# One reciprocal for the softmax sums of up to three head pairs, spread back through DRAM, in an attention plus two feed-forward kernel

## Chip, cores and metric

The kernel runs on one core of a Trainium2 chip. The metric is the device time in microseconds (us) of one execution, as the median of several runs; lower is better. The core has five engines that each work through their own list of instructions in order: TensorE (PE; its weight loads are listed apart as PEld), VectorE (DVE), ScalarE (ACT), GpSimd (POOL) and SyncE (SP), which here only issues DMA transfers. Engines wait for each other through semaphores.

## What is computed

```python
scores = q @ k.T / sqrt(64)                 # batch 2, 12 heads, 448 tokens, head size 64
scores = cap * tanh(scores / cap)
attn   = exp(scores - max(scores))          # the kernel leaves the max out: softmax does not depend on it
attn   = attn / (sum(attn) + 1e-9)
x = (attn @ v)                              # heads side by side: 896 tokens x 768
h = x @ w_in;  g = s * relu(h)**2 + b;  x = g @ w_out          # 768 -> 2048 -> 768
h = x @ w2_in; g = h * clip(h + 3, 0, 6) / 6; y = g @ w2_out   # 768 -> 2048 -> 768
```

## The kernel before

**Attention.** The 24 heads are taken in 12 pairs; pairs 0 to 5 belong to batch entry 0, pairs 6 to 11 to entry 1. A pair has four units, one for each block of 112 keys. For a unit n, `scores` (L211) writes keys by queries for both heads into a PSUM tile `ps`; `tanh` (L215) and `exps` (L220) on ACT make the tile `t` in SBUF; `attend` (L228) multiplies it with v and adds into the PSUM tile `pav` of the pair; `add_up` (L236) adds the four `t` of a pair into `acc`, the first add on POOL, the other two on DVE. `total` (L246) multiplies `acc` with a matrix of ones, so that all 64 rows of a head in the PSUM tile `pz` hold the same sums over the keys. `invert` (L251) takes the reciprocal of the whole tile, 128 rows by 448, into `rb`; `scale_x` (L255) multiplies `pav` with it; `split_x` (L260, L261) parts the product into a rounded half `xh` and a rest `xl`, which the feed-forward products need.

**Feed-forward.** `products` (L100) multiplies every weight block three times (rest of w by xh, w by xl, w by xh) into a PSUM tile `pf`. The weights come as 64-bit numbers in 68 chunks; each is fetched by SP (L57) into `raw`, then made into two fp32r halves by `rescale` (ACT, L64), `join` in three steps (DVE, L76, L78, L80), `upper` (ACT, L89) and `lower` (DVE, L95). The first two chunks are prepared beside the attention, one step every third unit (the table `early`).

**Order.** The order of instructions on every engine is the order in which the code is written (`manual_schedule`); the loop over n is a software pipeline. At step n it issues `scores(n+2)`, `exps(n)`, `tanh(n+1)`, then, where n is 4p+6, `total(p)` and `invert(p)`, then `attend(n-1)` and `add_up(n-1)`, and at n = 4p+8 `scale_x(p)` and `split_x(p)`. From n = 47 on it also issues two pieces of the feed-forward a step; a piece is three matmuls. The first twelve pieces (half of two weight chunks) read x of batch entry 0 only; the next twelve read x of entry 1, pair 6 first, pair 11 sixth. The joins of the third chunk are issued beside the first twelve pieces. SP's queue holds the loads of q and k (L203) of the pairs to come and the fetches of weights, in the order of the code. The buffers that matter: `pav` 3, `pz` 1, `t` 6, `acc` 2, `rqk` 3.

Of the kernel before, what the change touches and what calls it, by code (L numbers as in the profile page):

```python
# [7 lines left out]
F32 = mybir.dt.float32  # L8
# [15 lines left out]
WARM = 2  # L24
SCALE = 1.0 / D**0.5


@with_exitstack
def attention_moe_moe(ctx: ExitStack, tc: tile.TileContext, qk, v, cap, w1i, w1o, s, b, w2i, w2o, out):
    nc = tc.nc  # L30
    const = ctx.enter_context(tc.tile_pool(name="const", bufs=1))
# [9 lines left out]
    zeros = tp.tile([128, S], F32, name="zeros", tag="h")  # L41
    ones = const.tile([QT, D], F32, name="ones")
    x = [[act.tile([128, KD, S], F32R, name=f"x{p}{bi}") for p in ("h", "l")] for bi in range(B)]
# [205 lines left out]
    def invert(p):
        rb[p] = at.tile([128, S], F32, name="rb", bufs=2)  # L250
        nc.vector.reciprocal(rb[p], sums.pop(p)[:, :S])  # L251

    def scale_x(p):
        xf[p] = at.tile([128, S], F32, name="xf", bufs=2)
        nc.vector.tensor_mul(xf[p], pav.pop(p)[:, :S], rb.pop(p))  # L255

    def split_x(p):
        bi, hp = divmod(p, H // 2)
        hi, lo = (t[:, hp, :] for t in x[bi])
        nc.vector.tensor_copy(hi, xf[p])  # L260
        nc.vector.tensor_sub(lo, xf.pop(p), hi.bitcast(F32))  # L261

    with tc.manual_schedule():
# [24 lines left out]
        early = {6 + 3 * j: step for j, step in enumerate(steps + [(rescale, 2)])}  # L288

        fill, ps_f = None, None  # L290
        has = lambda n: 0 <= n < N
        for n in range(-2, N + 5):
# [71 lines left out]
```

## Time and profile before

| | us |
|---|---|
| median of 3 runs (lowest, highest) | 586.85 (586.08, 587.51) |
| the profiled execution | 586.05 |
| its span, first to last instruction | 584.3 |
| attention, until the feed-forward runs alone | about 0 to 124 |
| feed-forward alone | about 124 to 584 |

| engine | busy us | share of the span |
|---|---|---|
| PE | 569.6 | 97% |
| DVE | 403.1 | 69% |
| ACT | 272.7 | 47% |
| POOL | 31.1 | 5% |

How to read it: a share over the whole span mixes the two stages, so the stage of the attention is read by itself, from the waits and the lists in order of time. Times in those lists count from the start of the span. In a row, the bracket at the end gives the idle time of the engine before the instruction and what ended it. An instruction of DVE can begin while the last one still drains, so the time that one costs its queue is the distance between two starts, a little less than its own length.

### The profile page before, as it was taken

The numbers are of one execution on the slowest core, as the hardware profiler recorded it, in microseconds if no ns is written. First come the engines' busy times: TensorE is split into PE (matmuls) and PEld (weight loads), VectorE is DVE, ScalarE is ACT, GpSimd is POOL, SyncE is SP. The second block draws the span as 40 slices with busy tenths as digits, with TensorE's granted clock in tenths as the row PEclk, the third lists the DMA queues.
The fourth block names the chain that finished last, engine by engine and source line by source line (L and its number), as shares of the span: only waits on it lengthen the run. The fifth ranks groups of instructions, "written<-read, shape, count | busy, mean of one in ns | idle before, by whom it ended". The sixth has DMA issues, their size and how long they took to land.

```text
span 584.3 us, 6908 instructions
## 1 busy us (share of the span) xinstructions
PE 569.6 (97%) x2740; PEld 459.7 (79%) x2740; DVE 403.1 (69%) x521; ACT 272.7 (47%) x386; POOL 31.1 (5%) x16
## 2 busy tenths in 40 slices
PE   7998898999999999999999999999999999999997
PEld 2222222489999999999999999999999999999996
DVE  1699999998777777564456457888888864455420
ACT  6988878455555555223222325555555522321210
POOL 1221423100000000000000000000000000000000
PEclk9999999999999999999999999999999999999999
DMA  8903220033333323432343323333332344433200
GB/s 266 274 31 118 63 70 16 1 108 109 108 109 108 109 90 109 145 97 90 102 146 92 115 100 108 109 108 109 108 109 91 108 145 130 161 116 121 67 33 31
DMA packets 14097, 61.77 MB, mean 106 GB/s; under 512 B 1826, under 2 KB 3618, under 8 KB 13842
## 3 DMA queue, kind: packets, MB, share of 16 engines
q1 hardware_dynamic: 13920, 61.12, 32.1%
q8 instruction: 21, 0.34, 0.2%
q10 hardware_dynamic: 146, 0.23, 0.1%
q14 instruction: 10, 0.08, 0.0%
HBM read 58.59 MB, written 2.75 MB: 105 GB/s over the span
## 4 chain that ended last, share of the span: by engine, by line
PE 79%; DVE 13%; ACT 5%; issue 2%; DMA 1%; ACTq 0%; DVEq 0%
PE pf L100 78%; DVE acc L236 5%; DVE rb L251 5%; ACT t L215 2%; ACT t L220 2%; DVE xf L255 1%; DMA rqk<-in_qk 1%; DVE xh L260 1%; DVE w L80 0%; DVE w L78 0%; DVE xl L261 0%; PE ps L211 0%; PE pz L246 0%; DVE wlo L95 0%; ACT raw L64 0%
## 5 line engine op out<-in xcount | busy, mean ns | idle before, releaser
L100 PE MATMUL pf<-xh,wlo 128*128 128x448 f32 x384 | 140.7, 366 | 0.0
L100 PE MATMUL pf<-xl,whi 128*128 128x448 f32 x384 | 140.3, 365 | 0.2 <-DVE xl L261 0.2
L100 PE MATMUL pf<-gh,whi 128*128 128x448 f32 x384 | 140.2, 365 | 0.0
L100 PE MATMUL pf<-gl,whi 128*128 128x448 f32 x384 | 140.2, 365 | 0.0
L100 PE MATMUL pf<-xh,whi 128*128 128x448 f32 x384 | 140.2, 365 | 0.0
L100 PE MATMUL pf<-gh,wlo 128*128 128x448 f32 x384 | 140.2, 365 | 0.0
L89 ACT CAST whi<-w 128x768 fp32r<-128x768 f32 (+1 forms) x68 | 54.2, 798 | 175.1 <-PE pf L100 96.8
L95 DVE TENSOR_TENSOR wlo<-w,whi 128x768 fp32r<-128x768 f32 (+1 forms) x68 | 61.6, 906 | 82.9 <-ACT whi L89 82.9
L100 PEld LDWEIGHTS pf<-xh,wlo 128*128 128x128 f32 x384 | 72.1, 188 | 8.6 <-issue 2.8
L100 PEld LDWEIGHTS pf<-xl,whi 128*128 128x128 f32 x384 | 72.1, 188 | 6.1 <-DVE xl L261 0.5
L100 PEld LDWEIGHTS pf<-gh,whi 128*128 128x128 f32 x384 | 72.1, 188 | 5.7
L100 PEld LDWEIGHTS pf<-gl,whi 128*128 128x128 f32 x384 | 72.1, 188 | 5.7
L100 PEld LDWEIGHTS pf<-xh,whi 128*128 128x128 f32 x384 | 72.1, 188 | 5.7
L100 PEld LDWEIGHTS pf<-gh,wlo 128*128 128x128 f32 x384 | 72.1, 188 | 5.7
L78 DVE SCALAR_TENSOR_TENSOR w<-raw,w 128x768 uint32<-128x768 uint32 (+1 forms) x68 | 61.9, 911 | 2.3
L80 DVE SCALAR_TENSOR_TENSOR w<-raw,w 128x768 uint32<-128x768 uint32 (+1 forms) x68 | 61.9, 911 | 2.3
L64 ACT ACTIVATE raw<-raw 128x768 f32<-128x768 f32 (+1 forms) x68 | 58.8, 865 | 0.0
L211 PE MATMUL ps<-rqk 64*112 64x448 f32 x192 | 48.2, 580 | 1.8 <-ACT t L215 1.0
L215 ACT ACTIVATE t<-ps 112x896 f32<-112x896 f32 x48 | 43.5, 907 | 12.4 <-PE ps L211 12.4
L236 DVE TENSOR_TENSOR acc<-acc,t 112x896 f32<-112x896 f32 x24 | 41.3, 1721 | 10.3 <-POOL acc L236 9.2
L220 ACT ACTIVATE t<-t 112x896 f32<-112x896 f32 x48 | 45.6, 949 | 1.4
L228 PE MATMUL pav<-t,va 112*64 112x448 f32 x192 | 46.1, 559 | 0.0
(35 smaller groups left out, 355.2 us busy)
## 6 DMA issues: line engine op xcount, KB each, us to landing
raw<-in_w1i SPq DMA_DIRECT2D x16, 768.0 KB, 4.2
raw<-in_w2i SPq DMA_DIRECT2D x16, 768.0 KB, 4.3
raw<-in_w1o SPq DMA_DIRECT2D x12, 768.0 KB, 4.2
raw<-in_w2o SPq DMA_DIRECT2D x12, 768.0 KB, 4.3
rqk<-in_qk SPq DMA_DIRECT2D x11, 448.0 KB, 4.4
raw<-in_w1o SPq DMA_DIRECT2D x6, 512.0 KB, 3.8
raw<-in_w2o SPq DMA_DIRECT2D x6, 512.0 KB, 3.9
out<-y SPq DMA_DIRECT2D x12, 224.0 KB, 1.9
```

The source lines that it names most:

```text
L64: nc.scalar.activation(up, up, AF.Copy, scale=2.0**-112)
L78: nc.vector.scalar_tensor_tensor(out=bits, in0=up, scalar=0x80000000, in1=bits, op0=ALU.bitwise_and, op1=ALU.bitwise_or)
L80: nc.vector.scalar_tensor_tensor(out=bits, in0=low, scalar=29, in1=bits, op0=ALU.logical_shift_right, op1=ALU.bitwise_or)
L89: nc.scalar.copy(ready[i][0][:, :n], whole[i][:, :n])
L95: nc.vector.tensor_sub(lo[:, :n], whole.pop(i)[:, :n], hi[:, :n].bitcast(F32))
L100: nc.tensor.matmul(ps[:, :S], w[a][:, sl], rhs[r], start=(k == 0 and i == 0), stop=(k == n_k - 1 and i == 2))
L211: nc.tensor.matmul(ps[:, j, :S], raw_qk[p][rows, 1, c * QT:(c + 1) * QT], raw_qk[p][rows, 0, :], start=True, stop=True)
L215: nc.scalar.activation(u_t[n], u_ps.pop(n)[:, :, :S], AF.Tanh, scale=icap_r)
L220: nc.scalar.activation(u_t[n], u_t[n], AF.Exp, scale=cap_r)
L228: nc.tensor.matmul(pav[p][D * j:D * j + D, :S], va[bi][:, 2 * hp + j, c, :], u_t[n][:, j, :], start=(c == 0), stop=(c == NQ - 1))
L236: (nc.gpsimd if c == 1 else nc.vector).tensor_add(acc[p], u_t.pop(n - 1) if c == 1 else acc[p], u_t[n])
L251: nc.vector.reciprocal(rb[p], sums.pop(p)[:, :S])
```

## The change

- The pairs are put in groups of 3, 3, 3, 2 and 1 (`GROUPS`). `total` multiplies `acc` with a matrix that has ones only in every n-th column (`pick`), and the pairs of a group add into the same `pz`: row i of a head's 64 rows holds the sums of pair i modulo n. One reciprocal then serves the whole group (`invert`, 5 instead of 12).
- The reciprocals of a group lie in n rows for each head. Two DMA transfers on SP write these rows to DRAM, and two more read them back, each repeated over 64 partitions, into a tile `rb` of 128 x (n x 448). For the group of one nothing is spread.
- `take` copies `pav` to an SBUF tile `xu` as soon as the pair's products are complete, at n = 4p+6. `pav` has 2 buffers instead of 3.
- `finish_x` multiplies in place and makes xh and xl. For the pairs of a group whose last pair is q it is issued at n = 4q+8, 4q+10 and 4q+12, for the last group at n = 51.
- The first add of a pair's four units goes to DVE too. POOL only fills `pick` at the start.

```diff
+GROUPS = [(0, 3), (3, 3), (6, 3), (9, 2), (11, 1)]
...
-    ps_v = tc.alloc_tile_pool(name="ps_v", bufs=3, space=PSUM)
+    ps_v = tc.alloc_tile_pool(name="ps_v", bufs=2, space=PSUM)
...
-        (nc.gpsimd if c == 1 else nc.vector).tensor_add(acc[p], u_t.pop(n - 1) if c == 1 else acc[p], u_t[n])
+        nc.vector.tensor_add(acc[p], u_t.pop(n - 1) if c == 1 else acc[p], u_t[n])
...
+            nc.tensor.matmul(sums[p0][D * j:D * j + D, :S], pick[:, PICKS.index((n, p - p0)), :], acc[p][:, j, :], start=(p == p0), stop=(p == p0 + n - 1))
...
+    def take(p):
+        xu[p] = at.tile([128, S], F32, name="xu", bufs=5)
+        nc.vector.tensor_copy(xu[p], pav.pop(p)[:, :S])
+    def invert(p0):
+        n = group[p0][1]
+        rz[p0] = at.tile([128, S], F32, name="rz", bufs=2)
+        nc.vector.reciprocal(rz[p0], sums.pop(p0)[:, :S])
+        if n == 1:
+            rb[p0] = rz[p0]
+            return
+        rows = dram.tile([2, n, S], F32, name="rows", bufs=2)
+        wide = at.tile([128, 3, S], F32, name="rb", bufs=2)
+        for j in range(2):
+            nc.sync.dma_start(rows[j], rz[p0][D * j:D * j + n, :])
+        for j in range(2):
+            nc.sync.dma_start(wide[D * j:D * j + D, :n, :], rows[j:j + 1].to_broadcast([D, n, S]))
+        for r in range(n):
+            rb[p0 + r] = wide[:, r, :]
+    def finish_x(p):
...
+        xf = xu.pop(p)
+        nc.vector.tensor_mul(xf, xf, rb.pop(p))
+        nc.vector.tensor_copy(hi, xf)
+        nc.vector.tensor_sub(lo, xf, hi.bitcast(F32))
...
             if part == 0 and 0 <= done < P:
                 total(done)
-                invert(done)
+                if done == sum(group[done]) - 1:
+                    invert(group[done][0])
             if has(n - 1):
                 attend(n - 1)
                 add_up(n - 1)
-            if part == 2 and 0 <= done < P:
-                scale_x(done)
-                split_x(done)
+            if part == 0 and 0 <= done < P:
+                take(done)
+            for p in finishes.get(n, ()):
+                finish_x(p)
```

The line numbers of the changed kernel are higher: L240 is the add, L258 `take`, L263 the reciprocal, L270 and L272 the transfers to DRAM and back, L280 to L282 `finish_x`; L78, L80, L82 and L97 are the joins and `lower` that were L76, L78, L80 and L95. PE's list of instructions is the same but for `pick`, and ACT's is the same.

DVE's list around the reciprocal of the third pair, before:

```order
L251 RECIPROCAL rb<-pz 128x448
L236 TENSOR_TENSOR acc<-acc,t 112x896
L80 SCALAR_TENSOR_TENSOR w<-raw,w 128x768
L236 TENSOR_TENSOR acc<-acc,t 112x896
L255 TENSOR_TENSOR xf<-pav,rb 128x448
L260 CAST xh_74<-xf 128x448
L261 TENSOR_TENSOR xl_75<-xf,xh_74 128x448
L251 RECIPROCAL rb<-pz 128x448
```

And after:

```order
L263 RECIPROCAL rz<-pz 128x448
L240 TENSOR_TENSOR acc<-t 112x896
L258 COPY xu<-pav 128x448
L240 TENSOR_TENSOR acc<-acc,t 112x896
L82 SCALAR_TENSOR_TENSOR w<-raw,w 128x768
L240 TENSOR_TENSOR acc<-acc,t 112x896
L280 TENSOR_TENSOR xu<-xu,rb 128x448
L281 CAST xh_74<-xu 128x448
L282 TENSOR_TENSOR xl_75<-xu,xh_74 128x448
L240 TENSOR_TENSOR acc<-t 112x896
L258 COPY xu<-pav 128x448
L280 TENSOR_TENSOR xu<-xu,rb 128x448
```

A third add and the copy of `pav` have come in behind the reciprocal, the first multiplication by `rb` stands behind them, and the adds of the next pair but one stand behind that multiplication.

SP's list from the load of v for batch entry 1 (`va_95`) on, before:

```order
L274 DMA va_95<-in_v 112x3072
L203 DMA rqk<-in_qk 128x896 x4
L57 DMA raw<-in_w1i 128x1536
L203 DMA rqk<-in_qk 128x896 x4
L57 DMA raw<-in_w1i 128x1536
L203 DMA rqk<-in_qk 128x896
```

And after (`va_97` is the same load):

```order
L295 DMA va_97<-in_v 112x3072
L207 DMA rqk<-in_qk 128x896 x3
L270 DMA rows<-rz 3x448 x2
L272 DMA rb<-rows 64x1344 x2
L207 DMA rqk<-in_qk 128x896
L59 DMA raw<-in_w1i 128x1536
L207 DMA rqk<-in_qk 128x896 x2
L270 DMA rows<-rz 3x448 x2
```

The four small transfers of a group stand in the same queue as the loads; the load of the next pair's q and k comes behind them.

DVE's list at the end of the attention, from the reciprocal of pair 10 (here the sums of pairs 9 and 10), before:

```order
L251 RECIPROCAL rb<-pz 128x448
L236 TENSOR_TENSOR acc<-acc,t 112x896 x2
L255 TENSOR_TENSOR xf<-pav,rb 128x448
L260 CAST xh_76<-xf 128x448
L261 TENSOR_TENSOR xl_77<-xf,xh_76 128x448
L76 TENSOR_SCALAR w<-raw 128x768
L78 SCALAR_TENSOR_TENSOR w<-raw,w 128x768
L80 SCALAR_TENSOR_TENSOR w<-raw,w 128x768
L251 RECIPROCAL rb<-pz 128x448
L95 TENSOR_TENSOR wlo<-w,whi 128x768
L255 TENSOR_TENSOR xf<-pav,rb 128x448
L260 CAST xh_76<-xf 128x448
```

And after, from the first multiplication by the spread `rb` on:

```order
L280 TENSOR_TENSOR xu<-xu,rb 128x448
L281 CAST xh_76<-xu 128x448
L282 TENSOR_TENSOR xl_77<-xu,xh_76 128x448
L78 TENSOR_SCALAR w<-raw 128x768
L80 SCALAR_TENSOR_TENSOR w<-raw,w 128x768
L82 SCALAR_TENSOR_TENSOR w<-raw,w 128x768
L263 RECIPROCAL rz<-pz 128x448
L258 COPY xu<-pav 128x448
L280 TENSOR_TENSOR xu<-xu,rb 128x448
L281 CAST xh_76<-xu 128x448
L282 TENSOR_TENSOR xl_77<-xu,xh_76 128x448
L280 TENSOR_TENSOR xu<-xu,rz 128x448
```

The last reciprocal, that of pair 11, has moved behind the multiplication of pair 9, which reads what the DMA brings; behind it now stand a copy and the work on two pairs (10 and 11) instead of one, and `lower` has moved to the end.

## Rows read from the trace of the kernel before

**Rows 1.** The page, busy us (share of the span) xinstructions.

```profile
PE 569.6 (97%) x2740; PEld 459.7 (79%) x2740; DVE 403.1 (69%) x521; ACT 272.7 (47%) x386; POOL 31.1 (5%) x16
```

**Rows 2.** PE's waits, 20 to 110 us: us in total, times, longest.

```profile
PE pz L246 <- DVE acc L236: 7.4, 7, 1.5
```

**Rows 3.** PE in order of time: start us, us, instruction [idle before].

```profile
1.39 3.35 PE L280 MATMUL pz<-zeros 128*128 128x448 f32 x4 [1.39 <-DVE zeros L275]
...
19.48 0.97 PE L246 MATMUL pz<-acc,ones 112*64 112x448 f32 x4
...
35.81 0.97 PE L246 MATMUL pz<-acc,ones 112*64 112x448 f32 x4
...
99.56 0.97 PE L246 MATMUL pz<-acc,ones 112*64 112x448 f32 x4 [1.01 <-DVE acc L236]
107.89 0.97 PE L246 MATMUL pz<-acc,ones 112*64 112x448 f32 x4 [1.08 <-DVE acc L236]
...
123.89 0.47 PE L100 MATMUL pf<-xl,whi 128*128 128x448 f32 x1 [0.19 <-DVE xl L261]
```

**Rows 4.** DVE in order of time, same columns, in the attention.

```profile
20.50 2.96 DVE L251 RECIPROCAL rb<-pz 128x448 f32<-128x448 f32 x1 [5.54 <-PE pz L246]
23.38 2.22 DVE L236 TENSOR_TENSOR acc<-acc,t 112x896 f32<-112x896 f32 x2
25.52 0.61 DVE L255 TENSOR_TENSOR xf<-pav,rb 128x448 f32<-128x448 f32 x1
...
59.01 3.92 DVE L236 TENSOR_TENSOR acc<-acc,t 112x896 f32<-112x896 f32 x2
62.86 0.61 DVE L255 TENSOR_TENSOR xf<-pav,rb 128x448 f32<-128x448 f32 x1
63.50 0.39 DVE L260 CAST xh<-xf 128x448 fp32r<-128x448 f32 x1
63.93 0.63 DVE L261 TENSOR_TENSOR xl<-xf,xh 128x448 fp32r<-128x448 f32 x1
64.47 2.95 DVE L251 RECIPROCAL rb<-pz 128x448 f32<-128x448 f32 x1
67.34 1.03 DVE L236 TENSOR_TENSOR acc<-acc,t 112x896 f32<-112x896 f32 x1
68.28 0.55 DVE L76 TENSOR_SCALAR w<-raw 128x768 uint32<-128x768 uint32 x1
```

**Rows 5.** DVE in order of time, end of the attention.

```profile
116.00 0.55 DVE L76 TENSOR_SCALAR w<-raw 128x768 uint32<-128x768 uint32 x1
...
117.58 0.96 DVE L80 SCALAR_TENSOR_TENSOR w<-raw,w 128x768 uint32<-128x768 uint32 x1
118.46 2.95 DVE L251 RECIPROCAL rb<-pz 128x448 f32<-128x448 f32 x1
...
123.21 0.62 DVE L261 TENSOR_TENSOR xl<-xf,xh 128x448 fp32r<-128x448 f32 x1
```

**Rows 6.** A load of four bytes and the DVE instruction that waits for it.

```profile
0.73 0.52 ACTq L264 DMA_DIRECT2D capt<-in_cap  x1
...
1.97 0.15 DVE L281 RECIPROCAL icap<-capt 1x1 f32<-1x1 f32 x1 [0.56 <-DMA capt<-in_cap]
```

**Rows 7.** The page, DMA issues: xcount, KB each, median us to landing.

```profile
raw<-in_w1i SPq DMA_DIRECT2D x16, 768.0 KB, 4.2
...
out<-y SPq DMA_DIRECT2D x12, 224.0 KB, 1.9
```

**Rows 8.** Short stretches, per engine busy us; last PEclk, DMA share, GB/s.

```profile
21.00:21.50 0.50, 0.50 (x4) 0.27 (x4) 0.50 (x1) 0.50 (x1) 0.00 (x0) 1.00 1.07 246
21.50:22.00 0.50, 0.50 (x4) 0.00 (x0) 0.50 (x1) 0.50 (x2) 0.00 (x0) 1.00 0.72 172
...
120.50:121.00 0.50, 0.50 (x4) 0.47 (x3) 0.50 (x1) 0.50 (x2) 0.00 (x0) 1.00 0.92 381
```

**Rows 9.** The page, granted TensorE clock in 40 slices, tenths.

```profile
PEclk9999999999999999999999999999999999999999
```

More of the change, by code (lines that the diff above doesn't have):

```diff
@@ L25 @@
 SCALE = 1.0 / D**0.5
+GROUPS = [(0, 3), (3, 3), (6, 3), (9, 2), (11, 1)]
+PICKS = [(n, r) for n in (1, 2, 3) for r in range(n)]
 @with_exitstack
@@ L41, in attention_moe_moe @@
     zeros = tp.tile([128, S], F32, name="zeros", tag="h")
-    ones = const.tile([QT, D], F32, name="ones")
+    pick = const.tile([QT, len(PICKS), D], F32, name="pick")
     x = [[act.tile([128, KD, S], F32R, name=f"x{p}{bi}") for p in ("h", "l")] for bi in range(B)]
@@ L187, in attention_moe_moe @@
     at = tc.alloc_tile_pool(name="at", bufs=3)
-    ps_v = tc.alloc_tile_pool(name="ps_v", bufs=3, space=PSUM)
+    dram = ctx.enter_context(tc.tile_pool(name="dram", bufs=2, space=bass.MemoryType.DRAM))
+    ps_v = tc.alloc_tile_pool(name="ps_v", bufs=2, space=PSUM)
     ps_z = tc.alloc_tile_pool(name="ps_z", bufs=1, space=PSUM)
@@ L192, in attention_moe_moe @@
     N, P = len(units), B * H // 2
-    raw_qk, u_ps, u_t, acc, pav, sums, rb, xf = {}, {}, {}, {}, {}, {}, {}, {}
+    group = {p: (p0, n) for p0, n in GROUPS for p in range(p0, p0 + n)}
+    raw_qk, u_ps, u_t, acc, pav, xu, sums, rz, rb = {}, {}, {}, {}, {}, {}, {}, {}, {}
     va = [at.tile([QT, H, NQ, D], F32, name=f"va{bi}", bufs=1) for bi in range(B)]
@@ L242, in total @@
     def total(p):
-        sums[p] = ps_z.tile([128, 512], F32, name="pz")
+        p0, n = group[p]
+        if p == p0:
+            sums[p0] = ps_z.tile([128, 512], F32, name="pz")
         for j in range(2):
-            nc.tensor.matmul(sums[p][D * j:D * j + D, :S], ones, acc[p][:, j, :], start=True, stop=True)
+            nc.tensor.matmul(sums[p0][D * j:D * j + D, :S], pick[:, PICKS.index((n, p - p0)), :], acc[p][:, j, :], start=(p == p0), stop=(p == p0 + n - 1))
         acc.pop(p)
[L249 to L257, printed above, removed]
+    def take(p):
[17 more added lines that the diff above has]
+    def finish_x(p):
         bi, hp = divmod(p, H // 2)
         hi, lo = (t[:, hp, :] for t in x[bi])
-        nc.vector.tensor_copy(hi, xf[p])
-        nc.vector.tensor_sub(lo, xf.pop(p), hi.bitcast(F32))
+        xf = xu.pop(p)
+        nc.vector.tensor_mul(xf, xf, rb.pop(p))
+        nc.vector.tensor_copy(hi, xf)
+        nc.vector.tensor_sub(lo, xf, hi.bitcast(F32))
     with tc.manual_schedule():
@@ L275, in attention_moe_moe @@
         nc.vector.memset(zeros, 0.0)
-        nc.vector.memset(ones, 1.0)
+        nc.gpsimd.memset(pick, 0.0)
+        for i, (n, r) in enumerate(PICKS):
+            nc.gpsimd.memset(pick[:, i, r::n], 1.0)
         nc.scalar.activation(three, zeros[:, :1], AF.Tanh)
@@ L288, in attention_moe_moe @@
         early = {6 + 3 * j: step for j, step in enumerate(steps + [(rescale, 2)])}
+        finishes = {}
+        for p0, n in GROUPS:
+            for r in range(n):
+                finishes.setdefault(4 * (p0 + n - 1) + 6 + (2 + 2 * r if n > 1 else 1), []).append(p0 + r)
         fill, ps_f = None, None
```

## Prediction

> **What bounds the kernel now.** I read the page's engine shares first: PE is busy for 97% of the span, DVE for 69%, POOL for 5% [rows 1]. So the feed-forward stage, which this change does not touch, is PE work without gaps, and anything to be won lies where PE waits. Its waits in the attention come next: in 20 to 110 us PE waits 7.4 us, in seven pieces of at most 1.5 us, and all of them are `pz` (L246, `total`) waiting for DVE's last add into `acc` [rows 2]. PE in order of time shows what a pair costs without that wait: the first and the third `total` start at 19.48 and 35.81, so 8.15 us a pair; the tenth and eleventh start 8.33 apart with 1.08 of waiting, so 7.25 without it, since `scores` has run out there [rows 3]. DVE in order of time shows why PE waits: two adds beside POOL's add take 62.86 - 59.01 = 3.85 us, and 25.52 - 23.38 = 2.14 when POOL is still; a reciprocal takes 2.87 of the queue (64.47 to 67.34) [rows 4]. That makes 3.85 + 2.87 + 1.61 (xf, xh, xl, 62.86 to 64.47) = 8.3 us a pair, and with a weight step nearly every pair DVE is over PE's 8.15. The stage ends at 123.89, where PE's second matmul on pair 11 waits for that pair's xl, which starts at 123.21 and takes 0.62 [rows 3, 5]. From there on nothing waits, so the time of the kernel moves with the end of pair 11's xl, 123.83 now.
>
> **What the change takes away.** Seven reciprocals of 2.95 and POOL's adds go; 12 adds and 12 copies of `pav` come to DVE. An add of this shape costs 0.94 in the queue (67.34 to 68.28) and 1.03 to 1.1 to its end [rows 4]. No row shows DVE copying out of PSUM; between the 0.39 of xh (SBUF only) and the 0.62 of xl or xf I take 0.54, xl's distance to its follower, since xf also reads PSUM and has the long time [rows 4]. A pair then costs DVE three adds (3.1), a copy (0.54), 1.61 and about 5/12 of a reciprocal (1.2), 6.45 us, well under PE's 8.15. If DVE waited for nothing else, PE's 7.4 us would go: `total` of pair 10 would start at 35.81 + 7 x 8.15 + 7.25 = 100.1 instead of 107.89. Filling `pick` costs nothing: POOL has until the first `total` at 19.48. Two `pav` buffers instead of three cost nothing either, as long as the copy of a pair comes before the `attend` of the pair after next, three steps later.
>
> **What the change adds: a wait in DVE's queue.** Let P be the start of the group's last `total`. The reciprocal starts at P + 1.02 and lasts 2.95 (19.48 to 20.50) [rows 3, 4], so SP sends the rows off at P + 4.0. Writing 5 KB to DRAM: the store of y, 224 KB, lands after 1.9 us [rows 7], a load of four bytes lets its reader go after 1.24 [rows 6]; I take 1.4, nearer to the small one. Reading back: 2 x 64 x 5,376 = 688 thousand bytes. A `raw` fetch of 786 thousand lands after 4.2 us [rows 7] and runs at 381 GB/s once it is going [rows 8], so some 2.2 us of it are fixed; the store of y leaves 1.3 in the same way; I take 1.9. The rate is the open number. Long rows of separate memory into all partitions ran at that; the load of v in short pieces ran at 172 to 246 [rows 8]. The read-back has long rows, but 64 readers of one stretch of DRAM, and each transfer fills half of the partitions; no row has either. I take 220, the v load, because only rows that share neither oddity show more. That gives 3.1 us, and `rb` lands at R = P + 4.0 + 1.4 + 0.1 + 1.9 + 3.1 = P + 10.5.
>
> The Trainium skill ("SBUF — State Buffer", section on the DMA port swizzle) says that partitions 0 to 63 reach only half of the ports of a DMA, 218 GB/s at most; it speaks against two transfers of 64 partitions, and "DMA: Bandwidth & Descriptors" advises one of 128. By it the sum would be the one I take, by the `raw` rows the first rival below; no row here shows a 64-partition load.
>
> DVE gets to the first multiplication by `rb` at P + 8.0 (reciprocal, 0.94, 0.54, 2.14, and a weight step in each of the three groups). So it stands idle for some 2.5 us, and behind it in the queue stand the adds that PE's next `total` but one needs: 1.61, 0.94, 0.54, 1.61 and 2.2 to the end of the adds, 6.95 us. PE wants them at P + 16.3 (two pairs):
> - group 1: 10.5 + 6.95 - 16.3 = 1.1 us of waiting;
> - group 2 has a join (0.88, 117.58 to 118.46) [rows 5] between: 2.0;
> - group 3: PE wants them at 8.15 + 7.25 = 15.4: 2.0.
>
> So 5.1 of the 7.4 us come back, and `total` of pair 10 starts at 105.2. The SP queue holds the next load of q and k behind the read-back, some 7 us later than now; its pair is needed at P + 15.4, so that is hidden, with about 4 us to spare.
>
> **The end of the stage.** DVE first finishes pair 8 (1.61 after the adds), so the reciprocal of pairs 9 and 10 starts at 106.75. The trip is 0.05 + 1.4 + 0.05 + 1.9 + 2.1 (459 thousand bytes at 220), and pair 9 begins 2.95 + 5.5 = 8.45 later, at 115.2. Then 1.61, the three joins 2.46 (116.00 to 118.46) [rows 5], the reciprocal of pair 11 2.87, copy 0.54, pair 10 1.61, pair 11 1.7: xl of pair 11 ends at 126.0 against 123.83. PE, which could take up pair 10's piece 14.8 after its `total` of pair 10 (123.89 - 107.89 less the piece before it), would be idle for some 4 us. The sum is 105.2 - 107.89 = -2.7 at `total` of pair 10 and +4.9 behind it: **+2.2 us**. On the profiled execution of 586.05 that is 588.2; the median of the runs stands 0.8 higher, at 586.85, so **589.0**.
>
> **Rivals.**
> - *The read-back runs at full rate* (381 GB/s as the `raw` rows [rows 8]). R is P + 9.1; the waits are 0, 0.6 and 0.65, `total` of pair 10 starts at 101.35, pair 9's work 7.5 after a reciprocal at 102.9, and xl of pair 11 ends at 121.2: -2.6, **584.2**, not slower. For it: packets of 5 KB, near those of `raw`. Near 280 GB/s the change comes to nothing.
> - *The trip is hidden* (it lands before P + 8): no waits, xl ends at 118.8, -5.0, **581.8**. Against it: 4.1 us from the end of the reciprocal is less than the 4.2 that one fetch of like size takes.
> - *The one stretch of DRAM is a bottleneck* (half of the v rate, 110 GB/s): R is P + 13.6, the waits 4.2, 5.1 and 5.2, the end 2 us later still: +13.7, **600.5**. Nothing in the trace excludes it.
> - *The clock falls while PE waits at the end.* Now PE never waits over 1.5 us here [rows 2] and the granted clock is full in every slice [rows 9]; then it would be idle for 4. The first matmuls of the kernel, after idleness, took 3.35 us for four [rows 3], against 0.97 for four of `total`, side by side. If a stretch as long as that ran at half speed, 1.7 us more: **590.7**. The Trainium skill ("TensorE: Matmul & The Clock Gate") has such a fall to 1.2 GHz after idleness; no row here shows one.
> - The copy at 0.39 or 0.64 instead of 0.54 moves the end by some 0.5 us either way, the write at 1.24 or 1.9 by about -0.7 and +2.
>
> **Numbers.** The forecast has 0.35, the clock 0.12, the slow stretch 0.12, the full rate 0.23, the hidden trip 0.05, rates between forecast and full rate that end within 0.2% 0.13. About 0.2% (1.2 us) is what a measurement of this kernel can tell from no change. From the cases: slower 0.55 (the forecast's lower edge falls within 0.2%), same 0.18, faster 0.27. The range 583.5 to 597 leaves out the hidden trip and the slow stretch at its price.
>
> **What would show it.** DVE's waits should show the first multiplication (L280) waiting for `rb` by DMA, 2 to 3 us in each of three groups and about 2 in the fourth; DVE busy should fall from 403 to about 388 us, with adds of 1.1 us and no POOL. PE should wait for `acc` in three places (1.1, 2, 2) instead of seven, `total` of pair 10 should start near 105, and PE should wait about 4 us for pair 10's xl and 1 for pair 11's. A read-back that lands in 3.7 us makes the first rival, one above 7 us the third; matmuls of the feed-forward that start over 0.3 us apart behind the wait, the fourth. The forecast is wrong altogether if PE's waits for `acc` do not come back, or if something waits that I have not named, such as `scores` for its load.

## Result and the profile after

The changed kernel takes 593.47 us in the median (591.15 to 601.71) against 586.55 for the kernel before in the same series: 1.0099 times as long, with a 95% interval from 1.008 to 1.0118, so 5.8 us slower. The forecast was 2.2 us slower. Now and then an execution of any of these kernels has its whole feed-forward slowed; the comparisons leave out most such runs (those of e2, e4 and e7 still hold some), and of the profiles that fell on one (e2, e5, e7, e12, e16) only the attention is read. The profiled execution took 594.09, its span is 592.3, so it is 8.0 us longer than the one before.

The page of the kernel after, first its line on the engines (as [rows 1]), then the granted clock in 40 slices (as [rows 9]):

```profile
PE 577.1 (97%) x2740; PEld 463.1 (78%) x2740; DVE 385.8 (65%) x537; ACT 272.5 (46%) x386; POOL 1.1 (0%) x11
...
PEclk9999989899999999999999999999999999999999
```

DVE has lost 17 us of work and POOL all of its 30, as foreseen (388 for DVE), and the kernel is slower. PE is 7.5 us longer busy with the same matmuls, and two slices of the clock are no longer full. That is the first sign of a cost that the forecast did not have in these places.

The trip of the first group, kernel after: SP's issues, then DVE in order of time (start us, us, instruction, idle time before):

```profile
41.01 0.61 SPq L270 DMA_DIRECT2D rows<-rz  x2
42.30 1.14 SPq L272 DMA_DIRECT2D rb<-rows  x2
```

```profile
38.02 2.96 DVE L263 RECIPROCAL rz<-pz 128x448 f32<-128x448 f32 x1 [6.17 <-PE pz L252]
...
44.24 1.08 DVE L240 TENSOR_TENSOR acc<-acc,t 112x896 f32<-112x896 f32 x1
47.88 0.62 DVE L280 TENSOR_TENSOR xu<-xu,rb 128x448 f32<-128x448 f32 x1 [2.56 <-DMA rb<-rows]
```

The last `total` of the group starts at 37.00, so R is P + 10.9 (forecast P + 10.5): the write takes 1.3 us, the read-back 5.6 from its issue to the multiplication that waits for it. DVE stands idle for 2.56 us, and in the other three groups for 2.86, 2.32 and 2.06. A window of this read-back and one of the loads of 128 partitions that follow it in the same queue (busy us of PE, PEld, DVE, ACT, POOL; then granted clock, DMA share, GB/s):

```profile
44.50:47.50 3.00, 2.81 (x15) 0.76 (x12) 0.82 (x1) 2.97 (x5) 0.00 (x0) 1.00 0.99 228
48.00:51.00 3.00, 3.00 (x16) 0.91 (x16) 2.93 (x5) 2.26 (x4) 0.00 (x0) 1.00 0.96 388
```

PE's waits from 20 to 110 us, and PE in order of time, kernel after; these answer [rows 2] and [rows 3]:

```profile
PE pz L252 <- DVE acc L240: 6.5, 5, 2.5
```

```profile
55.00 0.97 PE L252 MATMUL pz<-acc,pick 112*64 112x448 f32 x4 [1.44 <-DVE acc L240]
63.12 0.97 PE L252 MATMUL pz<-acc,pick 112*64 112x448 f32 x4
...
81.93 1.19 PE L252 MATMUL pz<-acc,pick 112*64 112x448 f32 x4 [2.51 <-DVE acc L240]
91.70 0.97 PE L252 MATMUL pz<-acc,pick 112*64 112x448 f32 x4
...
109.45 1.40 PE L252 MATMUL pz<-acc,pick 112*64 112x448 f32 x4 [2.13 <-DVE acc L240]
...
128.13 0.47 PE L102 MATMUL pf<-xh,wlo 128*128 128x448 f32 x1 [1.97 <-DVE xh L281]
...
130.41 0.74 PE L102 MATMUL pf<-xl,whi 128*128 128x448 f32 x1 [0.19 <-DVE xl L282]
130.95 0.58 PE L102 MATMUL pf<-xh,whi 128*128 128x448 f32 x1
131.33 0.58 PE L102 MATMUL pf<-xh,wlo 128*128 128x448 f32 x1
```

The three waits stand where they were expected. What was not expected is what comes behind the longer ones. Behind the wait of 1.44 the next `total` comes 8.12 later, the natural pitch. Behind the wait of 2.51 it comes 9.77 later with no wait in between: 1.65 us are lost while PE works. From 130.95 to 133.57 the matmuls start 0.37 to 0.38 apart instead of 0.20. The clock shows why. Short stretches of the kernel after, in the same columns:

```profile
82.00:84.00 2.00, 2.00 (x8) 0.52 (x8) 1.93 (x4) 0.68 (x1) 0.00 (x0) 0.64 0.00 0
84.00:86.00 2.00, 2.00 (x6) 0.45 (x4) 2.00 (x4) 0.00 (x0) 0.00 (x0) 0.51 0.38 49
...
130.00:132.00 2.00, 1.81 (x5) 1.47 (x5) 2.00 (x4) 0.14 (x1) 0.00 (x0) 0.58 0.00 0
132.00:134.00 2.00, 2.00 (x7) 1.79 (x7) 1.93 (x4) 1.12 (x2) 0.00 (x0) 0.56 0.00 0
```

After PE had stood still for 2.5 us the chip granted the lower of its two levels (1.2 of 2.4 GHz, 0.5 in the row) for most of these 4 us; PE was busy all the time and did 14 entries in them. At the end it had stood still for 1.97 us and then three times for 0.19 to 0.29 before the clock fell.

The end of the attention, DVE in order of time (as [rows 5]):

```profile
119.61 0.62 DVE L280 TENSOR_TENSOR xu<-xu,rb 128x448 f32<-128x448 f32 x1 [2.06 <-DMA rb<-rows]
...
123.69 2.95 DVE L263 RECIPROCAL rz<-pz 128x448 f32<-128x448 f32 x1
...
129.74 0.63 DVE L282 TENSOR_TENSOR xl<-xu,xh 128x448 fp32r<-128x448 f32 x1
```

**Where the 8.0 us of the profiles are.** First `total` 20.76 against 19.48: +1.3. From there to `total` of pair 10, 88.69 against 88.41: +0.3. From that to the first matmul on the last xl, 20.96 against 16.00: +5.0. From that to the end, 461.9 against 460.4: +1.5, of which 1.3 lie before 133.86. The first item comes and goes: e10 and e3 (below) have the same code at the start, and their first `total` is at 20.45 and 19.61. Without it 6.7 us are left, near the 5.8 of the comparison.

### The profile page after: what moved, and what is told of

It is laid out like the page before. It is cut to its first block, busy times and chain, and to the rows that moved or that the text cites. A ratio compares the mean times of both kernels' runs of the same rounds, so it can differ in the third digit from the quotient of the medians.

```text
span 592.3 us, 6943 instructions
## 1 busy us (share of the span) xinstructions
PE 577.1 (97%) x2740; PEld 463.1 (78%) x2740; DVE 385.8 (65%) x537; ACT 272.5 (46%) x386; POOL 1.1 (0%) x11
## 4 chain that ended last, share of the span: by engine, by line
PE 89%; DVE 6%; DMA 4%; issue 0%; SPq 0%; ACTq 0%; ACT 0%; DVEq 0%
PE pf L102 79%; PE ps L215 4%; PE pav L232 4%; DMA rb<-rows 2%; DVE rz L263 2%; DVE acc L240 2%; PE pz L252 2%; DVE xl L282 1%; DVE xu L280 1%; DMA rqk<-in_qk 1%; DMA rows<-rz 1%; DVE xh L281 1%; DVE xu L258 0%; SPq L272 0%; DVE w L80 0%
## 5 line engine op out<-in xcount | busy, mean ns | idle before, releaser
L97 DVE TENSOR_TENSOR wlo<-w,whi 128x768 fp32r<-128x768 f32 (+1 forms) x68 | 61.7, 907 | 83.2 <-ACT whi L91 83.2
L80 DVE SCALAR_TENSOR_TENSOR w<-raw,w 128x768 uint32<-128x768 uint32 (+1 forms) x68 | 62.0, 911 | 2.3
L82 DVE SCALAR_TENSOR_TENSOR w<-raw,w 128x768 uint32<-128x768 uint32 (+1 forms) x68 | 61.9, 911 | 2.3
L215 PE MATMUL ps<-rqk 64*112 64x448 f32 x192 | 51.0, 616 | 1.0 <-DMA rqk<-in_qk 1.0
L219 ACT ACTIVATE t<-ps 112x896 f32<-112x896 f32 x48 | 43.5, 907 | 14.8 <-PE ps L215 11.1
L232 PE MATMUL pav<-t,va 112*64 112x448 f32 x192 | 47.7, 576 | 0.0
L215 PEld LDWEIGHTS ps<-rqk 64*112 64x112 f32 x192 | 14.5, 183 | 37.0 <-ACT t L224 14.8
```

Source lines behind the costliest of these rows:

```text
L80: nc.vector.scalar_tensor_tensor(out=bits, in0=up, scalar=0x80000000, in1=bits, op0=ALU.bitwise_and, op1=ALU.bitwise_or)
L82: nc.vector.scalar_tensor_tensor(out=bits, in0=low, scalar=29, in1=bits, op0=ALU.logical_shift_right, op1=ALU.bitwise_or)
L97: nc.vector.tensor_sub(lo[:, :n], whole.pop(i)[:, :n], hi[:, :n].bitcast(F32))
L215: nc.tensor.matmul(ps[:, j, :S], raw_qk[p][rows, 1, c * QT:(c + 1) * QT], raw_qk[p][rows, 0, :], start=True, stop=True)
L219: nc.scalar.activation(u_t[n], u_ps.pop(n)[:, :, :S], AF.Tanh, scale=icap_r)
L232: nc.tensor.matmul(pav[p][D * j:D * j + D, :S], va[bi][:, 2 * hp + j, c, :], u_t[n][:, j, :], start=(c == 0), stop=(c == NQ - 1))
```

## Experiments

Base is the changed kernel unless the diff is said to be against before. e14 and e15 ran once each (599.0 and 588.7 us); only their rows are used.

### Is it the wait for the read-back? (e1, e2)

e1 multiplies with `rz` itself (the sums of the wrong pairs); the transfers still run, but nobody waits for them.

```diff
-            rb[p0 + r] = wide[:, r, :]
+            rb[p0 + r] = rz[p0]
```

> The changed kernel with its four transfers per group still running, but finish_x multiplies by the reciprocals where they lie (rz) instead of the spread copy, so each row gets a wrong pair's sums and no DVE instruction waits for the read-back. Theory A (the read-back's wait in DVE's queue, with the clock falls that PE's waits bring, is all of the loss): PE's waits for acc in the groups go (1.4, 2.5, 2.1 us in the changed kernel), total of pair 10 starts near 100 instead of 109.5, pair 11's xl ends near 119, and the time is about 5 us below the kernel before: 581 to 583. Theory B (the loss is in what DVE and PE now do otherwise: the copy, the third add, two pav buffers, the long end of the list): the waits stay and the time stays within 2 us of the changed kernel, 591 to 594.

Measured: 0.9937 of before (0.9909 to 0.9965), some 3.7 us faster, and 9.5 us less than the changed kernel. PE's waits, 20 to 110 us, and the end:

```profile
PE pz L252 <- DVE acc L240: 0.4, 2, 0.2
```

```profile
100.34 0.92 PE L252 MATMUL pz<-acc,pick 112*64 112x448 f32 x4
...
116.79 0.47 PE L102 MATMUL pf<-xh,wlo 128*128 128x448 f32 x1 [1.54 <-DVE xh L281]
```

`total` of pair 10 starts at 100.34: DVE's relief is real and worth what the forecast said (100.1). All that the change loses, it loses to the waits for `rb`. But the forecast had priced them at 589.0 - 581.8 = 7.2 us, and they cost 9.5. What is left at the end is no wait for `rb`: PE waits 1.54 us for pair 10's xh, and the clock falls behind it (a window in the same columns as above):

```profile
118.00:120.00 2.00, 1.92 (x5) 1.13 (x5) 1.97 (x4) 0.00 (x0) 0.00 (x0) 0.50 0.00 0
```

e2 tests the rest: fillers, matmuls nobody reads, keep PE running up to the point where it will wait.

```diff
+                busy({4: 2, 7: 3, 10: 3}.get(done, 0))
                 total(done)
...
+        for _ in range(4):
+            next(fill)
+        busy(3)
```

> The changed kernel with 11 extra matmuls into an unused PSUM bank, issued on PE just before the three total that wait for DVE in the groups (2, 3, 3 of about 0.65 us) and before the piece that waits for pair 10 (3). Nothing is left out. Theory C (each of PE's waits also drops the granted clock, to 0.5 to 0.66 of full for about 3.5 us behind it, which costs 1.6 us at total of pair 7 and 1.6 us behind pair 11's xl): the clock stays at 1.0 in those stretches and the kernel, with more work, gets 2 to 4 us faster than the changed one: about 589 to 591. Rival: the low clock costs nothing that DVE's list would not have cost anyway: the same time or up to 2 us slower.

Measured: 1.0141 (1.007 to 1.0213), too wide to say anything about the time; its shortest run, 592.27 us, is above the 589 to 591 that were expected. The stretch behind pair 7's `total` says it, PE and then the windows:

```profile
81.84 0.97 PE L258 MATMUL pz<-acc,pick 112*64 112x448 f32 x4 [0.64 <-DVE acc L242]
89.96 0.97 PE L258 MATMUL pz<-acc,pick 112*64 112x448 f32 x4
```

```profile
82.00:84.00 2.00, 2.00 (x12) 0.60 (x10) 1.93 (x4) 0.60 (x1) 0.00 (x0) 1.00 0.04 8
84.00:86.00 2.00, 2.00 (x12) 0.47 (x8) 2.00 (x4) 1.45 (x2) 0.00 (x0) 1.00 0.52 49
```

DVE is as late as in the changed kernel (81.84 against 81.93), yet the next `total` comes 8.12 later instead of 9.77, at full clock: 24 entries in those 4 us instead of 14. At the end the fillers were too few: PE still waits 1.57 us for pair 10's xh (at 126.86), and the granted clock is 0.52 from 129 to 131.

### What does a wait of PE cost by itself? (e5, e6)

Here nothing of the change is in play: before, all adds on DVE (e3), and six needless half-size additions on DVE, ahead of the last add of pair 7 (e5) or one in each of pairs 2 to 7 (e6).

```diff
+HOLD = {31: 6}    # e6: {11: 1, 15: 1, 19: 1, 23: 1, 27: 1, 31: 1}
...
+    def hold(n, k):
+        for _ in range(k):
+            nc.vector.tensor_add(spare, u_t[n][:, 0, :], u_t[n][:, 1, :])
...
                 attend(n - 1)
+                hold(n - 1, HOLD.get(n - 1, 0))
                 add_up(n - 1)
```

> The kernel before with all adds on DVE (run e3, 582.7 us) and six additions of 112x448 into an unused tile on DVE ahead of the last add of pair 7, and nothing else: 6 x 0.54 = 3.2 us of delay at one place (0.54 is the queue time of an xl, which has this size). Theory of the clock: PE waits some 3 us for acc of pair 7, the granted clock falls behind that wait, and the next total comes 9.8 us after it instead of 8.15, as in the changed kernel behind 81.93: 582.7 + 3.0 + 1.6 = 587.3. Rival (a wait costs its own length and no more): the next total comes 8.15 later, clock full, 585.7.

> The same six additions as in e5, but one ahead of the last add of each of pairs 2 to 7: the same work on DVE, and no PE wait over 1.5 us. Theory of the clock: clock full in the attention, at most 582.7 + 3.2 = 585.9 and 1.6 us or more below e5 (DVE has some slack in pairs without a weight step, so less than 3.2 may arrive). Rival: the same time as e5 within 0.5 us.

Measured: 1.0018 (1.0008 to 1.0028) and 0.9977 (0.9967 to 0.9987): the same work costs 2.4 us more in one place. PE in order of time and one window, e5, then PE in e6:

```profile
82.52 1.76 PE L252 MATMUL pz<-acc,ones 112*64 112x448 f32 x4 [3.93 <-DVE acc L238]
93.00 0.97 PE L252 MATMUL pz<-acc,ones 112*64 112x448 f32 x4
```

```profile
84.00:86.00 2.00, 2.00 (x8) 0.53 (x6) 2.00 (x3) 0.00 (x0) 0.00 (x0) 0.50 0.01 3
```

```profile
46.38 0.97 PE L252 MATMUL pz<-acc,ones 112*64 112x448 f32 x4 [1.49 <-DVE acc L238]
54.55 0.97 PE L252 MATMUL pz<-acc,ones 112*64 112x448 f32 x4
```

The waits sum to 5.1 us in e5 and 4.6 in e6, so their length is nearly the same. The pitch behind the long one is 10.48, 2.36 over the natural 8.12; behind e6's longest, 1.49, it is 8.17. So here, without groups or transfers, a long wait costs its length and 2.4 us more; the rival, that it costs its length alone, falls.

The extra is not set by the length of the wait. Three `total` of e7 (below), each behind a wait of 1.81 or none:

```profile
47.81 0.97 PE L252 MATMUL pz<-acc,pick 112*64 112x448 f32 x4 [1.81 <-DVE acc L240]
...
85.67 0.97 PE L252 MATMUL pz<-acc,pick 112*64 112x448 f32 x4 [1.81 <-DVE acc L240]
95.38 0.97 PE L252 MATMUL pz<-acc,pick 112*64 112x448 f32 x4
```

Behind the first the granted clock stays at 1.00 and the next `total`, with a wait of 0.94, comes 9.13 later; behind the second it falls to 0.50 from 87 to 90, and the next comes 9.71 later without a wait, 1.6 over the natural 8.12. Two more waits of e7, 1.81 and 1.88, were followed by no fall. Behind a wait of 2.77 (e14) 3.05 us were lost, behind one of 2.46 (e16, with one of 2.03 shortly before it) 2.58, behind 2.51 (the changed kernel) 1.65.

### Why is the read-back slow? (e8, e9, e12, e14, e15)

The forecast left open whether the half of the partitions that each transfer fills or the one stretch of DRAM that all readers read would hold the rate. e8 and e14 read head 0's rows for both heads, e15 reads other numbers into all but two partitions, so x is scaled wrongly in these three; the bytes are the same.

```diff
-        for j in range(2):
-            nc.sync.dma_start(wide[D * j:D * j + D, :n, :], rows[j:j + 1].to_broadcast([D, n, S]))
+        nc.sync.dma_start(wide[:, :n, :], rows[:1].to_broadcast([128, n, S]))           # e8
...
+        for j in range(2):                                                              # e14
+            nc.sync.dma_start(wide[D * j:D * j + D, :n, :], rows[:1].to_broadcast([D, n, S]))
...
+        nc.sync.dma_start(wide[:, :n, :], rows[:, :n, :])          # e15: rows has 128 rows
...
+        nc.sync.dma_start(wide[:, :n, :], rows[:, None].to_broadcast([2, D, n, S]))     # e9
...
+        rows = dram.tile([16, n, S], F32, name="rows", bufs=2)                          # e12
+        for j in range(2):
+            nc.sync.dma_start(rows[8 * j:8 * j + 8].rearrange("g n s -> n g s"), rz[p0][D * j:D * j + n, None, :].to_broadcast([n, 8, S]))
+        nc.sync.dma_start(wide[:, :n, :], rows[:, None].to_broadcast([16, 8, n, S]))
```

> The changed kernel, but the read-back is one transfer into all 128 partitions with the rows of the first head for both (so the second head of a pair is scaled with the wrong sums): the same 688 thousand bytes, one issue less. If it was the 64 partitions of each transfer that held the rate at 194 to 251 GB/s, the rate goes to near 380 GB/s, the read-back takes 3.7 us instead of 4.9, DVE's waits for it fall from 9.8 to about 5 us, PE's for acc from 6.5 to under 3, and the kernel takes 587 to 589. If it was the one stretch of DRAM that all readers read, the rate and the time stay (593).

> The changed kernel with its two read-backs of 64 partitions, but both read the rows of head 0 (as e8 did in one transfer of 128). If the halves of the partitions hold the rate, it stays at that of the changed kernel: the read-back of group 1 lets DVE go some 5.5 us after its first issue, DVE waits 9 to 10 us for rb in all. If it is the number of different stretches that are read at a time (one in e8, two in the changed kernel, sixteen in e12), it is as fast as e8: 4.0 us, and 4 us of waiting.

> The changed kernel with one read-back into 128 partitions from 128 different rows of a DRAM tile (filled once from q at the start, the rows of the sums written into the first two; so x is scaled with other numbers, and the start is longer by 688 KB of traffic). Halves of the partitions: the rate of e8 and of the raw fetches, 380 GB/s or more, 4 us from issue to DVE. Number of stretches: that of e12 or less, 5.5 us or more.

Measured: DVE's first multiplication of group 1 and then a window of the read-back, for e8, e14 and e15 in this order:

```profile
46.35 0.62 DVE L279 TENSOR_TENSOR xu<-xu,rb 128x448 f32<-128x448 f32 x1 [1.01 <-DMA rb<-rows]
```

```profile
44.00:46.30 2.30, 2.11 (x12) 0.71 (x12) 1.34 (x2) 2.30 (x4) 0.00 (x0) 1.00 0.85 344
```

```profile
48.37 0.63 DVE L280 TENSOR_TENSOR xu<-xu,rb 128x448 f32<-128x448 f32 x1 [3.13 <-DMA rb<-rows]
```

```profile
44.50:47.50 3.00, 2.81 (x16) 0.76 (x12) 0.74 (x1) 2.97 (x5) 0.00 (x0) 1.00 0.99 217
```

```profile
46.75 0.63 DVE L280 TENSOR_TENSOR xu<-xu,rb 128x448 f32<-128x448 f32 x1 [1.49 <-DMA rb<-rows]
```

```profile
44.00:46.70 2.70, 2.51 (x14) 0.76 (x12) 1.27 (x2) 2.70 (x4) 0.00 (x0) 1.00 0.97 385
```

| | partitions | source | first issue to multiplication | DVE's waits for rb |
|---|---|---|---|---|
| after | 2 x 64 | 2 stretches | 42.30 to 47.88, 5.6 us | 9.8 us |
| e14 | 2 x 64 | 1 stretch | 42.22 to 48.37, 6.2 us | 10.9 us |
| e8 | 128 | 1 stretch | 42.33 to 46.35, 4.0 us | 4.0 us |
| e15 | 128 | 128 rows | 42.63 to 46.75, 4.1 us | 5.7 us |

With 64 partitions a transfer the rate is 217 to 228 GB/s, with 128 it is 344 to 385, whether one stretch is read or more. The slow kernels also have two transfers where the fast ones have one, but the DMA engines are busy for 0.99 of the slow windows, and the loads of 128 partitions that follow one another in the same queue run at 388. So in these four kernels it is the halves. The Trainium skill ("SBUF — State Buffer", Door 1: The DMA port swizzle) says that partitions 0 to 63 reach only 8 of the 16 ports and partitions 64 to 127 the other 8; these four kernels agree with it.

e8's profiled run took 587.10 us and its shortest 586.04, the time of before: with a read-back at this rate the change would gain nothing. The first rival had put that case at 584.2. Its end was right (19.8 us from `total` of pair 10 to the last xl, as worked out), but PE waits 2.43 us there for pair 10's xh, and the matmuls behind it run at the lower clock.

e9 and e12 were to bring the right rows in one transfer.

> The changed kernel with one edit: the two read-backs of a group become one transfer whose source repeats the rows of head 0 over partitions 0 to 63 and those of head 1 over 64 to 127 (e8 did that with the rows of one head only). Theory of the half partitions: the rate is that of e8 (377 to 394 GB/s), rb lands some 1.2 us sooner than in the changed kernel, DVE waits about 4 us for it instead of 9.8, PE about 2 for acc instead of 6.5, no fall of the clock before the end of the attention: 586 to 587.5, about the time of before. Rival: e8 was fast because all partitions read one head's rows; with two stretches the rate is that of the changed kernel, 593.

> The changed kernel with one read-back into 128 partitions and the right rows, as e9, but each group's rows lie 8 times for each head in DRAM, so that the outer step of the read-back counts 16 and not 2. In e9 the last 6 us of each read-back ran at 51 to 54 GB/s with a DMA share of 0.13, which is 2 of 16 engines: the two outer steps went to two engines. Theory of the half partitions: with 16 outer steps all engines work and both halves are filled at once; the trip is that of e8 plus up to 0.5 us for a write of 43 KB per head instead of 5: DVE waits 4 to 6 us for rb, PE 2 to 3.5 for acc, 586 to 589. Rival (not the halves but two stretches of DRAM were slow): 593 or more, as the changed kernel.

Both missed: 1.0906 (1.0856 to 1.0956) and 1.0332 (1.0288 to 1.0376). A stretch in e9 while DVE waits for group 1:

```profile
56.00:58.00 2.00, 0.00 (x0) 0.00 (x0) 0.00 (x0) 0.00 (x0) 0.00 (x0) 0.50 0.13 54
```

A DMA share of 0.13 is 2 engines of 16: the source's outer step counts 2, and the work seems to be dealt out by that step. DVE waited up to 16.7 us. In e12, with 16 outer steps, all engines are busy, but the write of eight copies takes 3.8 us (39.74 to 43.56) and the read-back runs at 249 GB/s:

```profile
45.50:48.50 3.00, 3.00 (x14) 0.75 (x12) 0.00 (x0) 2.93 (x4) 0.00 (x0) 1.00 1.01 249
```

Why e12 is slow although it fills 128 partitions stays open. So a full-rate read-back with the right rows was not found.

### What are the parts worth? (e3, e4, e7, e10, e11, e13, e16)

e3 is the kernel before with the first add on DVE, nothing else.

```diff
-        (nc.gpsimd if c == 1 else nc.vector).tensor_add(acc[p], u_t.pop(n - 1) if c == 1 else acc[p], u_t[n])
+        nc.vector.tensor_add(acc[p], u_t.pop(n - 1) if c == 1 else acc[p], u_t[n])
```

> The kernel before with one part of the change alone: the first add of each pair on DVE instead of POOL. By the rows of before, two adds beside POOL's take 3.85 us of DVE's queue, three alone 0.94 + 2.14 = 3.08, so DVE's list falls from 8.3 to 7.6 us a pair plus weight steps, just about PE's 8.15. Theory D (the adds are the good part of the change and the rest spends it): nearly all of PE's 7.4 us of waiting for acc goes and the time is 579 to 581, 6 to 7 us below the kernel before. Rival (the port is no matter, POOL's add is work taken off DVE): DVE gets 0.9 us more a pair, and the time is 590 or above.

Measured: 0.9929 (0.9912 to 0.9946), 4.2 us faster than before, as good as e1 but less than the 6 to 7 that were expected: 2.4 of PE's 7.4 us of waiting for `acc` stay. PE in e3:

```profile
102.85 0.97 PE L246 MATMUL pz<-acc,ones 112*64 112x448 f32 x4 [0.58 <-DVE acc L236]
...
119.40 0.47 PE L100 MATMUL pf<-xh,wlo 128*128 128x448 f32 x1 [0.99 <-DVE xh L260]
```

One line of the change is worth as much as the whole of it without its waits. What it removes is that two of DVE's adds take 3.85 us beside POOL's and 2.14 alone [rows 4]. The reciprocals saved do bring something more: from the first `total` to that of pair 10 e1 takes 80.65 us (19.69 to 100.34) and e3 83.24 (19.61 to 102.85). But e1 loses it at the end, with its wait of 1.54 and the clock behind it.

e7 takes every pair as a group of one: no transfers, but the copy.

```diff
-GROUPS = [(0, 3), (3, 3), (6, 3), (9, 2), (11, 1)]
+GROUPS = [(p, 1) for p in range(12)]
```

> The changed kernel with twelve groups of one: 12 reciprocals, no transfer, the copy out of PSUM and the adds on DVE stay. Against e3 (adds on DVE alone) this adds the copy, 0.54 us a pair, and the multiplication reads SBUF. With the copy DVE needs about 3.1 + 0.54 + 2.87 + 1.6 = 8.1 us a pair, and 8.9 where a weight step falls, against PE's 8.15. If the copy costs its queue time wherever DVE is behind: 2 to 4 us over e3, 584.7 to 586.7, PE waits for acc of 0.5 to 1 us in many pairs and none above 1.5. If the copy lies in slack: 582.7 as e3.

Measured: 1.013 (1.0108 to 1.0152), far above what was expected. DVE in e7:

```profile
36.68 1.09 DVE L240 TENSOR_TENSOR acc<-acc,t 112x896 f32<-112x896 f32 x1
...
38.84 2.96 DVE L263 RECIPROCAL rz<-pz 128x448 f32<-128x448 f32 x1 [0.21 <-PE pz L252]
```

The last add of a pair now stands next to the reciprocal that waits for PE's `total` of that add: 38.84 - 37.68 = 1.16 us in which DVE can do no more than a weight step. The pitch is 29.71 to 38.84, 9.13. In before and e3 the finish of the last pair lies between the two and covers this. So e7 measures an order, not the price of the copy, which has a queue time of 0.53 in the changed kernel (41.84 to 42.37), as forecast.

e4 lets the groups of three finish two steps later and takes pairs 9 to 11 one by one.

```diff
-GROUPS = [(0, 3), (3, 3), (6, 3), (9, 2), (11, 1)]
+GROUPS = [(0, 3), (3, 3), (6, 3), (9, 1), (10, 1), (11, 1)]
...
-... + (2 + 2 * r if n > 1 else 1), []).append(p0 + r)
+... + (4 + 2 * r if n > 1 else 1), []).append(p0 + r)
```

> The changed kernel with finish_x of the groups of three two steps later, so that the trip through DRAM is covered, and the pairs 9, 10 and 11 as groups of one, without a trip, at the end; xu has 6 buffers. Nothing is left out. Theory A: DVE's first multiplication still waits about 1 us, but no longer in front of adds that PE waits for; PE waits for acc at most 0.5 us in a group, the clock stays full, total of pair 10 starts near 101 and the time is 579 to 582. Theory B (DVE's new work is too much for the list whatever the DMA does): PE still waits for acc in several pairs, and the time is 587 or above.

Measured: 1.0003 (0.9969 to 1.0036), between the two theories. PE in e4:

```profile
94.05 0.97 PE L252 MATMUL pz<-acc,pick 112*64 112x448 f32 x4 [0.19 <-DVE acc L240]
104.80 1.26 PE L252 MATMUL pz<-acc,pick 112*64 112x448 f32 x4 [3.50 <-DVE acc L240]
```

Until 94.05 PE runs at its natural pitch with waits of 0.19 at most: finished late, three groups cost nothing. Then the finishes of pairs 6 to 8 and of the single pairs meet, and one wait of 3.50, with a fall of the clock behind it, takes the gain.

e10 is e3 with two joins of the third weight chunk moved behind pair 11's finish.

```diff
-        ... beside(0, iter(())))
+        ... [lambda: rescale(3), lambda: join(2, 0), lambda: None, lambda: None])
...
                 split_x(done)
+                if done == P - 1:
+                    join(2, 1)
+                    join(2, 2)
+                    upper(2)
+                    lower(2)
```

> The kernel before with all adds on DVE (e3), and the last two joins of the third weight chunk, its upper and its lower issued behind pair 11's finish instead of ahead of its reciprocal. PE's wait of 0.99 + 0.19 us for pair 11 (119.40 and 120.06 in e3) should go, since the reciprocal can start 1.9 us sooner: 582.7 - 1.2 = 581.5. Rival: the third chunk, due some 14.6 us after the first piece (24 pieces of 0.61), comes late and PE waits for wlo there: 582.7 or more.

Measured: 580.93 us, 0.9894 (0.9879 to 0.9909): 6.2 us faster than before, some 12 faster than the changed kernel, the best of all. Pair 11's xl starts 5.1 us after its `total` (112.61 to 117.71); in e3 it was 7.6 (111.77 to 119.38). PE no longer waits there.

e11, e13 and e16 add to e10 groups of three for pairs 0 to 5, finished later, with the read-back of e9, of e12 and of the changed kernel.

```diff
+GROUPS = [(0, 3), (3, 3)] + [(p, 1) for p in range(6, 12)]
...
+... + ((3 if p0 else 4) + 2 * r if n > 1 else 2), []).append(p0 + r)
```

> Grouping only where a late finish hides the trip: pairs 0 to 2 and 3 to 5 as groups of three with the one-transfer read-back of e9, finished one or two steps later than in the changed kernel; pairs 6 to 11 as in e10, each with its reciprocal and no copy. DVE has four reciprocals less in the first 60 us, six copies more: PE's waits for acc in pairs 3 to 6 of e3 (0.64 and 0.22) should go, those of pairs 7 to 10 shrink by what DVE is ahead (1.6 us in e3): 581.5 - 0.9 to 2.4 = 579.1 to 580.6. Rival: the finishes of pairs 3 to 5 pile up beside those of pair 6 and make a wait of over 2 us there, clock and all: 584 or more.

> As e11 (groups of three for pairs 0 to 5 with a late finish, pairs 6 to 11 as in e10) with the read-back of e12. Expected as for e11, from e10's 580.9: PE's waits for acc of e10 (0.64, 0.21, 0.30, 0.37, 0.31, 0.58) shrink by 0.9 to 2 us: 579 to 580. Rival: the finishes of pairs 3 to 5 pile up beside pair 6's and make a wait of over 2 us with the clock behind it: 584 or more.

> e11 and e13 with the changed kernel's own four transfers (write 1.27 us, read-back 5.5): pairs 0 to 2 and 3 to 5 as groups with a late finish, pairs 6 to 11 as in e10. If the finish comes after the trip, PE's waits of e10 in pairs 3 to 10 (2.4 us) shrink by 0.9 to 2: 579 to 580. If pairs 3 to 5 still wait for rb (their finish is one step sooner than that of pairs 0 to 2) or pile up with pair 6: 583 or more, with a wait of over 1.5 us near pair 6 or 7.

Measured: 1.0421 (1.0406 to 1.0436), 1.0049 (1.0034 to 1.0064), 0.9999 (0.9989 to 1.001), none as fast as e10. e11 has e9's two engines, e13 e12's long write (40.99 to 44.79). e16, DVE and then PE:

```profile
71.60 0.62 DVE L286 TENSOR_TENSOR xu<-xu,rb 128x448 f32<-128x448 f32 x1 [2.75 <-DMA rb<-rows]
```

```profile
81.67 1.76 PE L252 MATMUL pz<-acc,pick 112*64 112x448 f32 x4 [2.46 <-DVE acc L240]
92.37 0.97 PE L252 MATMUL pz<-acc,pick 112*64 112x448 f32 x4
```

The rival of e16 held: the second group still waits for `rb`, meets pair 6, PE waits, the clock falls (pitch 10.70). Whether a group finished late enough would gain on e10 was not settled.

## Why the prediction was off

The direction was right, and the mechanism with its places: DVE waits for the spread `rb` in four places, PE's waits for `acc` fall from seven to three that matter, the end of the stage is later, the load of q and k stays hidden. The size was off, 2.2 us forecast and 5.8 measured. By its own steps:

- **The trip.** P + 10.5 forecast, P + 10.9 measured in group 1: write 1.3 (forecast 1.4), read-back at 228 GB/s between 44.5 and 47.5 (220). Right.
- **PE's waits.** 1.1, 2.0, 2.0 forecast (5.1); 1.6, 2.5 and 2.3 measured, the first and the third with a second small wait of 0.18 one pair earlier (6.5 in all). The trip was 0.4, 0.3 and 0.1 longer than forecast in the three groups, the small waits add 0.4, and together they are most of the 1.4 us.
- **The price of a wait: the step that failed.** The sum took each wait at its length. The wait of 2.51 cost 1.65 more behind it, and those at the end 1.5 more behind 130.41. The forecast had this mechanism only as its fourth rival, for the end alone, "for an idle time of 4", at 1.7 us and a chance of 0.12; at the end it came true with 1.97 and three short waits. That waits of 2 us in the groups could do the same was not asked, although [rows 2] showed none over 1.5, so the full clock of [rows 9] was no evidence for longer ones. That its 1.7 came near is partly luck: it was taken from the kernel's first matmuls, whose stretch the trace of before shows at a granted clock of 1.00, and the price ranges from 1.3 to 3.1 in the runs. e2 shows that the loss goes when PE is kept running, e5 that it comes without groups and transfers too. The Trainium skill ("TensorE: Matmul & The Clock Gate", Part 1: The HAM clock gate) has a fall to 1.2 GHz after idleness; e5 shows one here, with a granted clock of 0.50 behind a wait of 3.93 us.
- **`total` of pair 10.** Forecast -2.7, measured +0.3 from the first `total`: -2.7 + 1.4 + 1.65 = +0.35.
- **The end.** +4.9 forecast, +5.0 measured. Right. PE stood idle for 1.97, 0.29 and two times 0.19, not for 4 and 1: it came to pair 10's piece 16.7 us after its `total` (109.45 to 126.16) and not 14.8, because the clock had fallen behind the wait of 2.13 (to 0.50 from 110 to 113). There that cost nothing, since DVE's list was later still.
- **What is left.** With 0.35 + 5.0 + 1.5 the sum is 6.8 us, against 5.8 measured in the comparison and 6.7 in the profile without its late start.
- **The rivals.** The full rate and the slow stretch (381 and 110 GB/s) are refuted by the 228 of the trace, and e8, where all partitions read one stretch at 344, shows that the stretch is no bottleneck. The hidden trip's 581.8 is near what e1 shows without the waits (582.15 in its shortest run). Two sums on the way are off by under 0.1 us: the terms to the end of the adds give 6.90 and not 6.95, those of R at the full rate 9.2 and not 9.1.

## What to carry to other kernels

When a change brings a new wait to an engine that feeds TensorE, work out each single idle time it makes there, not only the sum; where one is longer than any in the profile before, put a fall of the clock behind it into the forecast itself. In this case it cost 1.3 to 3.1 us beyond the wait where it came, and of waits between 1.5 and 1.9 us only some had one behind them. Before a cheaper operation is bought with a round trip, take the part of the change that costs nothing alone: here one add moved off POOL brought as much as the whole change without its waits. A transfer into half of the partitions ran at 217 to 228 GB/s here where one into all of them ran at 344 to 388 (249 in e12, unexplained), and one whose outer step counts 2 at 54.

## What was not expected of the hardware

- A PE wait of 3.93 us was followed by 2.36 us of extra time (e5), one of 2.51 by 1.65, one of 2.77 by 3.05 and one of 1.91 by 1.60 (both e14), while waits of 1.44 and 1.49 were followed by nothing (after at 55.00, e6 at 46.38), and of e7's four waits of 1.81 to 1.88 one was followed by 1.6 us and three by nothing.
- A DMA from DRAM into 128 partitions ran on 2 of 16 engines, at 54 GB/s, when the outer step of its source counted 2 (e9).
